# One early sigmoid on ScalarE, into a tile that nothing reads, in a fused linear-attention and gated-MLP kernel

## Chip, cores and metric

The kernel runs on one core of a Trainium2 chip. The time is device microseconds (us) from start to end of one execution; lower is better. Before the change it was 556.48 us, the median of 3 runs (555.26 to 557.22).

## What is computed

```python
# q, k, v, alpha: (4, 8, 768, 48); x below: (3072, 384); w_gate, w_val: (384, 1536); w_out: (1536, 384)
for t in range(S):
    state = alpha[:, :, t, :, None] * state + np.einsum('bhd,bhe->bhde', k[:, :, t], v[:, :, t])
    y[:, :, t] = np.einsum('bhd,bhde->bhe', q[:, :, t], state)
...
gate = 1.0 / (1.0 + np.exp(-(x @ w_gate)))
val = x @ w_val
return (gate * val @ w_out).astype(np.float32)
```

The first loop is a linear attention with decay, by batch and head. Its output, with the heads side by side, is the input x of a gated MLP whose gate is a sigmoid.

## The kernel before, in words

The 3072 tokens are cut into 6 groups of 512 (NG), the 8 heads into 4 pairs (NP): 24 attention units. The MLP's 1536 inner columns are cut into 12 slices of 128 (NF), so there are 6 x 12 = 72 steps. A step of `step(s)` runs 9 gate matmuls, 9 value matmuls (L225: three products of split high and low parts over three tiles of x) and 9 output matmuls into `po` (L643). Between them ScalarE computes `sg`, the sigmoid of the gate sums (L630), VectorE multiplies it into `pv` (L632), ScalarE rounds that to `hh` (L634), and VectorE forms the rest `hl` (L635).

In the first 12 steps the weights come in as well. `weight_piece` loads a piece of raw bits by DMA from the SyncE queue (L345), ScalarE makes two conversions in place (L347, L348), VectorE merges the bits (L351, twice), ScalarE writes the high part of `w` (L353) and VectorE the low part (L355). Raw buffers are used again, so a later L345 waits for an earlier L355. The attention units run in the same stretch: VectorE's scans G and F (L381, L385) and `dec` (L387), GpSimd's products with them (L388, L449), ScalarE's copies `kn` (L404) and sums of |F| (L393), VectorE's states `st` (L489), TensorE's small matmuls (L461, L466, L514, L520).

The order of the work is made ahead of time by the class `Plan`. Every piece of work is added with an engine, an estimated time, a key (a due step, or None) and the names that it reads and writes. `order()` then plays the pieces through and fixes the order in which each engine gets them. Among the pieces that an engine could begin, the one with the smallest rank goes first; the rank comes from the latest time at which a piece may begin:

```python
            by = min((latest[w] - 0.15 - time for w in users[n]), default=float("inf"))
            latest[n] = by if key is None else key * self.STEP if self.parts[n][6] and key > NF + 2 else min(by, key * self.STEP)
        rank = [t - 1000.0 if p[7] else t for t, p in zip(latest, self.parts)]
```

`users[n]` are the pieces that read what piece n writes, `p[7]` is the flag `soon`. On its own engine an instruction never overtakes the one ahead of it.

ScalarE's first piece is `picks` (L321 to L325): a zeroing ACTIVATE (function Copy, L322) and two copies, into `pick`, which TensorE's L508 reads. The functions used on ScalarE are Copy, Abs (L393) and Sigmoid (L630). The program contains two loads of an activation table, put there by the compiler: one ahead of L322, one ahead of the first sigmoid of L630.

The tiles of the pool `sb` are allocated in the order in which the function names them: ... `tiny`, `starts`, four `st`, `sg`, `between`, two `hh`, two `hl`, `every`, `one`.

Of the kernel before, what the change touches and what calls it, by code (L numbers as in the profile page):

```python
# [8 lines left out]
F32 = mybir.dt.float32  # L9
# [5 lines left out]
AF = mybir.ActivationFunctionType  # L15
ALU = mybir.AluOpType

P = 128
# [18 lines left out]
CH, EH = T // C, T // E  # L37
# [162 lines left out]
@with_exitstack  # L200
def gla_then_glu(ctx: ExitStack, tc: tile.TileContext, q, k, v, alpha, rows, vc, vh, weights_in, out):
    nc = tc.nc
    const = ctx.enter_context(tc.tile_pool(name="const", bufs=1))


    ident = const.tile([P, P], F32, name="ident")
    make_identity(nc, ident)
    flags = const.tile([P, NG * NP + 1], F32, name="flags")
    weights = Weights(const)
    within = const.tile([1, 1], I32, name="within")  # L210
    with ExitStack() as fast:
        chunked(fast, tc, rows, vc, vh, weights_in, out, const, ident, flags, weights, within)
        found = nc.values_load(within[0:1, 0:1], min_val=0, max_val=1)
    with tc.If(found < 1):
        general(tc, q, k, v, alpha, out, ident, weights)
# [13 lines left out]
def chunked(ctx, tc, rows, vc, vh, weights_in, out, const, ident, flags, weights, within):  # L229
    nc = tc.nc  # L230
    sb = ctx.enter_context(tc.tile_pool(name="sb", bufs=1))
    ps = ctx.enter_context(tc.tile_pool(name="ps", bufs=1, space=bass.MemoryType.PSUM))
    plan = Plan()
# [56 lines left out]
    d1f = sb.tile([P, T], F32, name="d1f")  # L290
    d1g = {n: sb.tile([P, T], BF16, name=f"d1g{n}") for n in (C, E)}
    mask = {n: sb.tile([P, n], F32, name=f"mask{n}") for n in (C, E)}
    tiny = sb.tile([P, EH], F32, name="tiny")
    starts = sb.tile([P, NG * NP, EH], F32, name="starts")
    sts = [sb.tile([P, EH + 1, D], F32, name=f"st{p}") for p in range(NP)]
    r_x = [const.tile([P, NK, 2, T], F32R, name="x0", tag="x0")]
# [24 lines left out]
    def picks():  # L321
        nc.scalar.activation(out=pick[:, :, 0:D], in_=d1f[:, 0:NK * D].rearrange("p (k m) -> p k m", m=D), func=AF.Copy, scale=0.0)  # L322
        for j in range(2):
            r = slice(R * j, R * j + R)
            nc.scalar.copy(out=pick[r, :, D:R], in_=ident[r, R * j:R * j + D].rearrange("p (k m) -> p k m", m=X16))  # L325

    plan.add("scalar", 0.7, None, picks, writes=[(pickn, "s")])
    plan.add("gpsimd", 1.5, NF - 4.0, later, writes=["later", *(("start", u) for u in range(EARLY))])

# [367 lines left out]
    for s in range(NG * NF):  # L697
        step(s)
        if s in finished:
# [11 lines left out]
                                                               func=AF.Abs, accum_out=flags[:, n_units:n_units + 1]),  # L711
# [6 lines left out]
        out=within, in0=total[1][0:1, 0:1], scalar1=G_BOUND, scalar2=None, op0=ALU.is_le), [total[0]])  # L718
# [150 lines left out]
```

## Time and profile before

| | |
|---|---|
| time, median of 3 runs | 556.48 us |
| range of the 3 runs | 555.26 to 557.22 us |
| time of the profiled execution | 556.98 us |
| its span | 555.3 us |
| instructions in it | 10288 |
| busy: PE / VectorE / ScalarE / GpSimd | 98% / 60% / 33% / 18% |

The profile is one execution taken by the hardware profiler. PE is TensorE's matmuls, PEld its weight loads, DVE VectorE, ACT ScalarE, POOL GpSimd, SP the SyncE queue. A line such as "41.11 0.60 ACT L630 ACTIVATE sg<-pg" gives the start in the span, the duration, the engine, the line of the kernel and the tiles; brackets give the idle time of the engine ahead of it and what ended that.

### The profile page before, as it was taken

To read this page: it belongs to the slowest core of one execution; us is meant where nothing else is said; L and a number is where in the kernel's file an instruction comes from. 1 tells how busy PE (TensorE), PEld (TensorE's weight loads), DVE (VectorE), ACT (ScalarE), POOL (GpSimd) and SP (SyncE) were. 2 spreads that over 40 slices of the span, in tenths; PEclk is the share of its full clock that TensorE was granted. 3 is DMA by queue.
4 is the path that set the end of the run, shared out by engine and by line. 5 is a ranking of instruction groups with operands and counts; after the bars stand their busy time and mean duration, and the time that the engine had idled before them with its cause. 6 is when DMAs were issued, how large, how long until landed. Compare 5 with 4: busy or idle time off the path is not lost.

```text
span 555.3 us, 10288 instructions
## 1 busy us (share of the span) xinstructions
PE 542.1 (98%) x4162; PEld 432.8 (78%) x4162; DVE 335.0 (60%) x648; ACT 183.9 (33%) x334; POOL 100.5 (18%) x133
## 2 busy tenths in 40 slices
PE   8999999999999999999999999999999999999994
PEld 4667776767888888888888888888888888888883
DVE  6889998899858457467467466476475342222221
ACT  2547767652322222322222322222332222221211
POOL 5711222142212112022022022022021010000000
PEclk9999999999999999999999999999999999999998
DMA  8537675644413213324124234024232011100001
GB/s 311 203 102 247 217 228 164 213 132 121 141 31 116 70 45 116 123 48 116 57 59 115 94 79 115 25 92 115 71 102 50 15 28 30 58 0 1 1 1 63
DMA packets 21449, 54.36 MB, mean 98 GB/s; under 512 B 3472, under 2 KB 8592, under 8 KB 21392
## 3 DMA queue, kind: packets, MB, share of 16 engines
q1 hardware_dynamic: 21392, 53.60, 31.6%
q8 instruction: 35, 0.57, 0.4%
q14 instruction: 22, 0.18, 0.1%
HBM read 41.01 MB, written 4.72 MB: 82 GB/s over the span
## 4 chain that ended last, share of the span: by engine, by line
PE 84%; DVE 6%; DMA 4%; ACT 3%; issue 1%; POOL 0%; SPq 0%; DVEq 0%; ACTq 0%; POOLq 0%
PE po L643 24%; PE pv L225 16%; PE pg L225 16%; PE at L225 15%; DMA raw<-in_w_dram 3%; PE pv L614 2%; PE at L560 2%; PE at L400 1%; PE pv L603 1%; PE at L567 1%; DVE w L355 1%; PE pg L603 1%; PE at L603 1%; DVE raw L351 1%; DMA first_w<-in_w_dram 1%
## 5 line engine op out<-in xcount | busy, mean ns | idle before, releaser
L225 PE MATMUL pg<-x,w 128*128 128x512 f32 x477 | 117.4, 390 | 0.0
L643 PE MATMUL po<-hh,w 128*128 128x512 f32 x432 | 115.7, 400 | 1.3 <-ACT hh L634 1.3
L225 PE MATMUL pv<-x,w 128*128 128x512 f32 x459 | 113.4, 391 | 0.7 <-DVE hl L635 0.7
L225 PEld LDWEIGHTS pg<-x,w 128*128 128x128 f32 x477 | 89.1, 188 | 19.1 <-issue 0.4
L225 PEld LDWEIGHTS pv<-x,w 128*128 128x128 f32 x459 | 85.5, 188 | 20.2 <-DVE hl L635 2.0
L643 PEld LDWEIGHTS po<-hh,w 128*128 128x128 f32 x432 | 78.2, 188 | 18.5 <-ACT hh L634 1.9
L225 PE MATMUL at<-x,w 128*128 128x512 f32 x360 | 88.3, 390 | 0.0
L225 PEld LDWEIGHTS at<-x,w 128*128 128x128 f32 x360 | 67.4, 188 | 14.2 <-issue 0.2
L591 POOL TENSOR_TENSOR vs<-st,dec 64x384 f32<-64x384 f32 x32 | 26.4, 827 | 213.0 <-DVE st L586 211.8
L643 PE MATMUL po<-hl,w 128*128 128x512 f32 x216 | 62.0, 392 | 0.0
L632 DVE TENSOR_TENSOR pv<-pv,sg 128x512 f32<-128x512 f32 x32 | 22.3, 697 | 53.9 <-PE pv L225 53.9
L388 POOL TENSOR_TENSOR in<-in,G 128x512 f32<-128x512 f32 x22 | 33.0, 1500 | 90.3 <-DVE G L381 42.1
L632 DVE TENSOR_TENSOR pg<-pg,sg 128x512 f32<-128x512 f32 x21 | 14.7, 699 | 56.2 <-PE pg L225 56.0
L643 PEld LDWEIGHTS po<-hl,w 128*128 128x128 f32 x216 | 40.2, 188 | 9.0 <-issue 0.4
L632 DVE TENSOR_TENSOR at<-at,sg 128x512 f32<-128x512 f32 x19 | 13.3, 699 | 53.0 <-PE at L225 53.0
L586 DVE SCALAR_TENSOR_TENSOR st<-st,dec,at 128x48 f32<-128x48 f32 x128 | 33.9, 265 | 8.4 <-PE at L567 3.0
L630 ACT ACTIVATE sg<-pg 128x512 f32<-128x512 f32 x32 | 19.2, 599 | 57.4 <-PE pg L225 57.4
L634 ACT CAST hh<-pv 128x512 fp32r<-128x512 f32 x32 | 18.9, 589 | 43.1 <-DVE pv L632 43.1
L630 ACT ACTIVATE sg<-at 128x512 f32<-128x512 f32 x21 | 12.6, 600 | 54.8 <-PE at L225 54.8
L630 ACT ACTIVATE sg<-pv 128x512 f32<-128x512 f32 x19 | 11.4, 600 | 52.5 <-PE pv L225 52.5
L381 DVE TENSOR_TENSOR_SCAN G<-in,d1g 128x512 f32<-128x512 f32 x22 | 26.7, 1215 | 2.0 <-DMA in<-in_rows_dram 1.8
L385 DVE TENSOR_TENSOR_SCAN F<-in,d1f 128x512 f32<-128x512 f32 x22 | 27.5, 1251 | 0.5
(158 smaller groups left out, 577.4 us busy)
## 6 DMA issues: line engine op xcount, KB each, us to landing
in<-in_rows_dram SPq DMA_DIRECT2D x16, 516.5 KB, 4.2
raw<-in_w_dram SPq DMA_DIRECT2D x12, 576.0 KB, 5.3
first_w<-in_w_dram SPq DMA_DIRECT2D x10, 576.0 KB, 5.0
x<-yt SPq DMA_DIRECT2D x30, 192.0 KB, 3.4
out_dram<-raw SPq DMA_DIRECT2D x18, 256.0 KB, 2.3
v<-in_vc_dram SPq DMA_DIRECT2D x22, 192.0 KB, 4.6
A<-in_rows_dram SPq DMA_DIRECT2D x32, 128.0 KB, 4.0
in<-in_rows_dram SPq DMA_DIRECT2D x4, 772.5 KB, 5.0
```

Of the source, the lines that this page charges most:

```text
L225: nc.tensor.matmul(out=dst, lhsT=lhs(a, i), rhs=rhs(b, i), start=(n == 0 and i == 0), stop=(n == len(todo) - 1 and i == NK - 1))
L381: plan.add("vector", scan(n), t["G"], lambda: nc.vector.tensor_tensor_scan(out=G[:, ::-1], data0=az[:, n:0:-1], data1=d1g[size], initial=0 ...
L385: plan.add("vector", scan(n), after(t["G"], 0.01), lambda: nc.vector.tensor_tensor_scan(out=F, data0=az[:, 0:n], data1=d1f, initial=0.0, o ...
L388: plan.add("gpsimd", pool_(n), t["kt"], lambda: nc.gpsimd.tensor_tensor(out=kT, in0=kT, in1=G, op=ALU.mult), [gn, (inn, "r")], [(inn, "k")])
L560: nc.tensor.matmul(out=pas[j][1][ro, c // 2 * E:(c // 2 + 1) * E], lhsT=kT[r, cs], rhs=A[r, j, cs], start=True, stop=True)
L586: nc.vector.scalar_tensor_tensor(out=st[:, c + 1, :], in0=st[:, c, :], scalar=dec[:, c:c + 1], in1=pas[c % 2][1][:, T // 2 + c // 2 * D:T ...
L591: plan.add("gpsimd", pool_(EH * D), t["sd"], lambda j=j: nc.gpsimd.tensor_tensor(out=vs[own[j], j], in0=st[own[j], 0:EH], in1=dec[own[j]]. ...
L603: nc.tensor.matmul(out=py[R * j:R * j + D, cs], lhsT=vs[r, j, c, :], rhs=A[r, j, cs], start=True, stop=True)
L630: plan.add("scalar", act(T), None, lambda: nc.scalar.activation(out=sg, in_=got["g"][1][:, 0:T], func=AF.Sigmoid), [got["g"][0]], [sgn], s ...
L632: plan.add("vector", vec(T), None, lambda: nc.vector.tensor_tensor(out=pv, in0=pv, in1=sg, op=ALU.mult), [sgn], [pvn], soon=soon)
L634: plan.add("scalar", act(T), None, lambda: nc.scalar.copy(out=hh, in_=pv), [pvn], [hhn], soon=soon)
L643: nc.tensor.matmul(out=pso_now[m][1][:, 0:T], lhsT=weights.part("o", b, f)[:, m * P:(m + 1) * P], rhs=h[a][:, 0:T], start=(f == 0 and i == ...
```

## The change

A tile `spot` of one column is allocated behind `tiny`, and a piece of work is added to the plan ahead of `picks`: a sigmoid of the first column of the constant tile `tiny` into `spot`, with key None, an estimated time of 0.1, the flag `soon`, and no names read or written. Nothing reads `spot`. All else stays; the lines behind it have numbers that are 1 higher.

```diff
-    tiny = sb.tile([P, EH], F32, name="tiny")
+    tiny, spot = sb.tile([P, EH], F32, name="tiny"), sb.tile([P, 1], F32, name="spot")
...
+    plan.add("scalar", 0.1, None, lambda: nc.scalar.activation(out=spot, in_=tiny[:, 0:1], func=AF.Sigmoid), soon=True)
     plan.add("scalar", 0.7, None, picks, writes=[(pickn, "s")])
```

## Rows read from the trace of the kernel before

**Rows 1.** The profile's page: the chain that ended last, its shares of the span by engine.

```profile
PE 84%; DVE 6%; DMA 4%; ACT 3%; issue 1%; POOL 0%; SPq 0%; DVEq 0%; ACTq 0%; POOLq 0%
```

**Rows 2.** The groups of instructions by line, ScalarE alone: count, busy time and mean ns of one, idle time before them and what ended it.

```profile
L322 ACT ACT_TABLE_LOAD x1 | 1.3, 1283 | 0.8 <-PEq L854 0.8
L630 ACT ACT_TABLE_LOAD x1 | 1.3, 1283 | 0.0
```

**Rows 3.** The chain that ended last, in order of time, around the second table load: start, length, what.

```profile
39.82 1.28 ACT L630
...
41.11 0.60 ACT sg L630
41.71 0.64 ACT raw L347
...
42.35 0.70 DVE pv L632
```

**Rows 4.** The timeline of ScalarE at the start of the span: start, length, instruction, idle time before it.

```profile
0.82 1.28 ACT L322 ACT_TABLE_LOAD   x1 [0.82 <-PEq L854]
2.11 0.32 ACT L322 ACTIVATE first_w<-d1f 128x144 f32<-128x144 f32 x1
2.34 0.45 ACT L325 COPY first_w<-ident 64x48 f32<-64x48 f32 x2
8.63 0.59 ACT L404 COPY kn<-at 128x512 f32<-128x512 f32 x1 [5.83 <-PE at L400]
...
10.31 0.19 ACT L393 ACTIVATION_READ_ACCUMULATOR F<-F 128x1 f32 x1
```

**Rows 5.** The timeline of all engines at the start: the memset of `tiny`, and the first matmuls that read `pick`.

```profile
1.72 0.07 DVE L310 MEMSET tiny<- 128x8 f32 x1
...
16.08 1.08 PE L508 MATMUL pg<-first_w 48*64 48x512 f32 x4
```

**Rows 6.** The timeline of ScalarE around the second table load.

```profile
39.07 0.73 ACT L353 CAST w<-first_w 128x576 fp32r<-128x576 f32 x1
39.82 1.28 ACT L630 ACT_TABLE_LOAD   x1
41.11 0.60 ACT L630 ACTIVATE sg<-pg 128x512 f32<-128x512 f32 x1
41.61 0.74 ACT L347 ACTIVATE raw<-raw 128x576 f32<-128x576 f32 x1
...
42.84 0.54 ACT L353 CAST w<-first_w 128x384 fp32r<-128x384 f32 x1
43.27 0.60 ACT L634 CAST hh<-pv 128x512 fp32r<-128x512 f32 x1
44.38 0.60 ACT L630 ACTIVATE sg<-pg 128x512 f32<-128x512 f32 x1 [0.51 <-PE pg L225]
```

**Rows 7.** The timeline of all engines in the same stretch: TensorE's, VectorE's and GpSimd's instructions, and the next load that SyncE issues.

```profile
37.19 2.30 PE L225 MATMUL pg<-x,w 128*128 128x512 f32 x9
...
39.91 2.34 PE L225 MATMUL pv<-x,w 128*128 128x512 f32 x9
...
40.87 3.55 SPq L345 DMA_DIRECT2D first_w<-in_w_dram  x2
...
41.89 0.53 DVE L351 SCALAR_TENSOR_TENSOR first_w<-first_w 128x384 uint32<-128x384 uint32 x1
42.05 1.52 POOL L449 TENSOR_TENSOR in<-in,F 128x512 f32<-128x512 f32 x1 [7.08 <-DVE F L385]
42.08 2.20 PE L225 MATMUL pg<-x,w 128*128 128x512 f32 x9
42.35 0.70 DVE L632 TENSOR_TENSOR pv<-pv,sg 128x512 f32<-128x512 f32 x1
42.96 0.64 DVE L387 TENSOR_TENSOR dec<-in,G 128x4 f32<-128x4 f32 x1
43.52 0.55 DVE L355 TENSOR_TENSOR w<-first_w,w 128x384 fp32r<-128x384 f32 x1
...
45.31 1.66 PE L643 MATMUL po<-hh,w 128*128 128x512 f32 x6
```

**Rows 8.** The timeline of VectorE: the same `dec` instruction with no GpSimd product beside it.

```profile
89.43 0.13 DVE L387 TENSOR_TENSOR dec<-in,G 128x4 f32<-128x4 f32 x1
```

**Rows 9.** The timeline of TensorE behind that stretch: the first instruction up to 135 us that has idle time ahead of it, and the four with the most.

```profile
54.24 1.66 PE L643 MATMUL po<-hh,w 128*128 128x512 f32 x6 [0.17 <-ACT hh L634]
56.20 2.33 PE L225 MATMUL pv<-x,w 128*128 128x512 f32 x9 [0.31 <-DVE hl L635]
...
88.05 0.56 PE L466 MATMUL at<-v,kn 128*48 128x48 f32 x16 [1.39 <-ACT kn L404]
...
108.94 0.73 PE L643 MATMUL po<-hh,w 128*128 128x512 f32 x2 [1.12 <-ACT hh L634]
...
119.98 0.66 PE L400 MATMUL at<-ident,in 128*128 128x128 f32 x4 [0.78 <-DVE st L489]
```

**Rows 10.** The page's costliest groups: the matmuls that read `hh`, `hl` and x, with count, busy time and mean ns of one.

```profile
L225 PE MATMUL pg<-x,w 128*128 128x512 f32 x477 | 117.4, 390 | 0.0
L643 PE MATMUL po<-hh,w 128*128 128x512 f32 x432 | 115.7, 400 | 1.3 <-ACT hh L634 1.3
...
L643 PE MATMUL po<-hl,w 128*128 128x512 f32 x216 | 62.0, 392 | 0.0
```

## The prediction

> **What bounds the kernel now.** I read the chain that ended last first, by engine and then in order of time around the second table load; then the table loads among ScalarE's groups; then the timelines of ScalarE, and of all engines in the same microseconds; last TensorE's idle times behind them. TensorE makes up 84% of the chain [rows 1], and it is in effect the bound: behind about 55 us it has few gaps and those are short [rows 9]. So whatever ScalarE saves counts only if it makes one of those gaps shorter, or if it starts a transfer or another engine earlier that does.
>
> ScalarE loads an activation table twice, at 0.82 us ahead of the zeroing of `pick`, and at 39.82 us ahead of the first sigmoid of the MLP, 1.28 us each [rows 2, 4, 6]. There is no third: the Copy and Abs work behind 39.82 runs on the table that the sigmoid asked for. The chain in order of time runs straight through the second load: load, sigmoid, L347, then VectorE's product L632 [rows 3]. Taken by itself that view says that 1.28 us of the span hang on the load. A chain names one releaser for each step, though, and not how far ahead the next-latest one was; that has to be read from the timelines of the neighbours [rows 7].
>
> **The change, part by part.**
>
> *Where the new sigmoid goes.* The rank of a piece is its latest start, less 1000 with `soon`. The new piece has key None and nobody uses what it writes, so its latest start is infinite, and infinite less 1000 is infinite. `picks` has users (L508 reads `pick`, and the chain of users ends in step 0 with key 0), so its rank is finite. Both can begin at once, so `picks` goes first. By this reading the sigmoid is not ScalarE's first instruction but the first one behind `picks`. The first load stays at 0.82 us, for Copy; the second moves from 39.82 us to the end of `picks`, 2.34 + 0.45 = 2.79 us [rows 4]. The number of loads is then two, as before. The rest of the plan stays as it is: the new piece takes 0.1 us of the plan's time on an engine that has nothing else ready there, reads and writes no name, and so displaces nothing.
>
> *What it adds at the start.* A load, 1.28 us, and a sigmoid of 128x1. No such sigmoid is in the trace; the nearest rows are a 128x1 instruction on ScalarE, 0.19 us, and an ACTIVATE of 128x144, 0.32 us [rows 4]. I take 0.2, the one-column row being nearest. The end is 2.79 + 1.28 + 0.2 = 4.3 us, 4.4 with the larger price. The next thing ScalarE does begins at 8.63 us, after 5.83 us of idling for TensorE [rows 4], so 4.2 us of cover are left. `tiny` is filled at 1.79 us, before the sigmoid can start, and `pick` is not read before 16.08 us [rows 5]. If the sigmoid did come first, the load would be the one at 0.82 us and `picks` would end 0.2 to 0.3 us later, still 13 us ahead of its reader. Cost on the path: 0 either way. A gain here is excluded too, as ScalarE is idle there already.
>
> *What it takes away at 39.82 us.* The load, 1.28 us. The cast ahead of it ends at 39.80 and the sigmoid starts at 41.11 [rows 6]; neighbours without a load overlap by 0.10 (the sigmoid runs 41.11 to 41.71, the next starts at 41.61), so ScalarE gets back 1.31 + 0.10 = 1.41 us. The sigmoid's input is there: the gate matmuls end at 37.19 + 2.30 = 39.49 [rows 7]. So it would start near 39.7. Now each thing that follows:
> - L632 waits for the value matmuls, whose end is 39.91 + 2.34 = 42.25, and stands on VectorE behind L351, which ends at 42.42 (instructions there overlap by some 0.07). It starts at 42.35 now [rows 7] and will then: gain 0.
> - L353 of `first_w` (42.84 now) needs that L351, so it starts at 42.45 at the earliest: up to 0.4 us gained on ScalarE. Its reader on VectorE, L355 at 43.52, stands behind `dec` L387, which takes 0.64 there against 0.13 alone [rows 7, 8] and ends at 43.60 as GpSimd's L449 ends at 43.57. That product was released by scan F, not by ScalarE. Gain for L355: 0. The load that SyncE issues behind it, whose issue ends at 40.87 + 3.55 = 44.42 [rows 7], does not move either.
> - `hh` L634 (43.27 now) needs L632, 42.35 + 0.70 = 43.05: 0.2 us gained. Its reader L643 starts at 45.31 because TensorE works through from 42.08 to there, 1.4 us after `hh` is done at 43.87 [rows 6, 7]. Gain: 0.
> - The second sigmoid waits for the gate matmuls, 42.08 + 2.20 = 44.28, after 0.51 us of idling [rows 6, 7]. It starts at 44.38 before and after. From there ScalarE is where it was.
>
> So the 1.41 us go into ScalarE's own waits between 39.8 and 44.4 us; at 44.38 the idle time is that much more and nothing has moved. TensorE's first gap behind this, 0.17 us at 54.24 [rows 9], is ten microseconds later.
>
> The rows show 1283 ns for a load and 1.31 us between the neighbours, with nothing else in it [rows 2, 6]. The Trainium skill, page "ScalarE: Activation LUTs", section "What ACT_TABLE_LOAD costs", counts a drain of 1380 ns on top and 2.66 us in all for a switch of sets. This trace does not show that drain. By the page ScalarE would get back 2.66 us instead of 1.41, and if all of that reached the end the time would be about 553.8 us. That lies with rival 2, whose chance holds it.
>
> *Sum.* Profiled execution: span 555.3, of which 0 goes and 0 comes; with the 1.7 us around the span that is 556.98 again. The median of the runs shown is 0.5 us below the profiled one, so 556.5 us. The bounds of the unknown part are 0 and 1.41 us gained.
>
> **Rivals.**
> 1. *The chain is right.* The load is on the path and all of the 1.41 us reach the end: 556.48 - 1.41 = 555.1 us, 0.25% less. For it: the chain view [rows 3]. Against it: four followers that are held by something else [rows 7], and a step of ScalarE that TensorE resets at 44.38 [rows 6].
> 2. *More than the load's row.* A slightly different timing in the first 12 steps lets TensorE's later gaps close. The five gaps listed sum to 0.17 + 0.31 + 1.39 + 1.12 + 0.78 = 3.8 us [rows 9]; half of that gives 554.6 us. For it: two of the largest wait for ScalarE. Against it: nothing of this change is left at 44.38 us that could reach them.
> 3. *Slower by placement.* `spot` is allocated between `tiny` and `starts`, so `sg`, `hh` and `hl` lie elsewhere. TensorE reads `hh` and `hl` in 432 + 216 = 648 matmuls all through the kernel. If the new place cost each of them the 10 ns by which the mean of those with `hh` (400) now exceeds those with x (390) [rows 10], that would be 6.5 us: 563.0. It decides the sign from 1.67 / 648 = 2.6 ns upwards. Against it: `hl` lies directly behind `hh` and reads at 392, so no place in this pool is seen to be dear, and a longer mean need not be a longer pace.
> 4. *The change doesn't do what it says.* Either the sigmoid stands behind `picks` (which I expect, and which is in the forecast), or a load is still made at L630: then 556.5 us, with 1.3 to 1.6 us more of ScalarE's idle start in use. Against the latter: only one load was made for 72 sigmoids with Copy and Abs between them [rows 2].
>
> **How the numbers follow.** About 0.3%, 1.67 us, is what a measurement of this kernel can tell from no change. Forecast (nothing reaches the end): 0.79. Rival 1: 0.08. Rival 2: 0.05. Rival 3: 0.06. Rival 4 with a load left at L630: 0.02. The forecast, rival 1 and rival 4 are all within 0.3%: 0.79 + 0.08 + 0.02 = 0.89. Faster is rival 2, 0.05; slower is rival 3, 0.06. The range takes in the full 1.41 us at its lower end, 555.0, and at the upper end as much as the runs shown differ among themselves above their median, some 1 us: 557.5. The cases outside it hold 0.11, and the spread of medians some more.
>
> **What would show it.** In the profile after: a table load at about 2.8 us behind `picks`, one at 0.82, none at L630; the first sigmoid of the MLP near 39.7 us; L632 still at 42.35, L355 still at 43.5, the second sigmoid still at 44.38 with TensorE's matmuls named as the releaser; TensorE's gaps at 54, 56, 88, 109 and 120 us as before; the matmuls that read `hh` and `hl` with means of 400 and 392. If the sigmoid stands first, there is one load in all and my reading of the rank is wrong, at no cost in time. If L632 or L355 moves ahead by a microsecond, the sum is wrong and rival 1 takes over; if the mean of L643 grows, rival 3.

## The result and the profile after

The changed kernel takes 561.0 us (median of 10 runs, 560.65 to 562.4) against 556.98 us for the kernel before (10 runs, 555.26 to 560.36): a ratio of 1.0078, 95% interval 1.0062 to 1.0095. It is slower, by some 4 us, and outside the forecast range. The profiled execution's span is 559.7 us, 4.4 more than before. TensorE's granted clock is 0.997 of full speed (the 2.4 GHz level) in both profiled executions, so the clock isn't the reason.

Everything that was forecast for ScalarE happened. The groups of ScalarE by line, then its timeline at the start (answers to [rows 2, 4]):

```profile
L322 ACT ACT_TABLE_LOAD x1 | 1.3, 1283 | 0.8 <-PEq L855 0.8
L327 ACT ACT_TABLE_LOAD x1 | 1.3, 1283 | 0.0
```

```profile
2.34 0.46 ACT L325 COPY first_w<-ident 64x48 f32<-64x48 f32 x2
2.81 1.28 ACT L327 ACT_TABLE_LOAD   x1
4.11 0.20 ACT L327 ACTIVATE spot<-tiny 128x1 f32<-128x1 f32 x1
9.28 0.58 ACT L405 COPY kn<-at 128x512 f32<-128x512 f32 x1 [4.97 <-PE at L401]
```

The sigmoid stands behind `picks`, not ahead of it; the load at L630 is gone, one at 2.81 us has come. Now the place where the load was, from the timeline of all engines (answers to [rows 6, 7]). This execution runs 0.65 us late from the first microseconds on, because 13 warm-up matmuls took 4.25 us (second fence) instead of 3.60, so 0.65 is to be taken off. It isn't the loss: the kernel e2 below, with the time of before, starts about as late (`kn` at 9.14 us; 8.63 before, 9.28 here).

```profile
40.35 0.61 ACT L631 ACTIVATE sg<-pg 128x512 f32<-128x512 f32 x1
...
42.37 0.75 ACT L348 ACTIVATE raw<-raw 128x576 f32<-128x576 f32 x1 [1.41 <-DMA raw<-in_w_dram]
...
43.00 0.70 DVE L633 TENSOR_TENSOR pv<-pv,sg 128x512 f32<-128x512 f32 x1
...
44.20 0.56 DVE L356 TENSOR_TENSOR w<-first_w,w 128x384 fp32r<-128x384 f32 x1
...
45.03 0.60 ACT L631 ACTIVATE sg<-pg 128x512 f32<-128x512 f32 x1 [0.38 <-PE pg L225]
```

```profile
4.55 4.25 PE L615 MATMUL pv<-ident 128*128 128x512 bf16 x13
```

The first sigmoid starts at 39.70 on the old scale instead of 41.11, VectorE's product at 42.35 as before, L356 at 43.55 (43.52), the second sigmoid at 44.38 as before, released by TensorE. The 1.41 us went into a wait of 1.41 us for a raw piece: the conversion behind the sigmoid (L347, now L348), which the prediction's list of followers left out, starts at 41.72 on the old scale against 41.61.

The loss is elsewhere. The page's costliest groups (answers to [rows 10]):

```profile
L225 PE MATMUL pg<-x,w 128*128 128x512 f32 x477 | 118.0, 392 | 0.0
L644 PE MATMUL po<-hh,w 128*128 128x512 f32 x432 | 117.5, 404 | 0.4 <-ACT hh L635 0.4
...
L644 PE MATMUL po<-hl,w 128*128 128x512 f32 x216 | 63.4, 397 | 0.0
```

The output matmuls take 4 and 5 ns more, those with x 1 to 2. By the pages the busy time grew by 1.8 us (hh), 1.4 us (hl) and 2.0 us (x: pg, pv, at), 5.2 us in all. TensorE's timeline of one step in the last group, first before, then after:

```profile
488.46 1.52 PE L643 MATMUL po<-hh,w 128*128 128x512 f32 x6
489.82 0.84 PE L643 MATMUL po<-hl,w 128*128 128x512 f32 x3
490.50 2.20 PE L225 MATMUL pv<-x,w 128*128 128x512 f32 x9
492.54 2.20 PE L225 MATMUL at<-x,w 128*128 128x512 f32 x9
494.58 1.52 PE L643 MATMUL po<-hh,w 128*128 128x512 f32 x6
```

```profile
486.43 1.56 PE L644 MATMUL po<-hh,w 128*128 128x512 f32 x6
487.83 0.86 PE L644 MATMUL po<-hl,w 128*128 128x512 f32 x3
488.53 2.24 PE L225 MATMUL at<-x,w 128*128 128x512 f32 x9
490.61 2.20 PE L225 MATMUL pg<-x,w 128*128 128x512 f32 x9
492.65 1.56 PE L644 MATMUL po<-hh,w 128*128 128x512 f32 x6
```

From start to start a step takes 6.12 us before and 6.22 after. The differences of the starts give its blocks: six matmuls with `hh` 1.36 and 1.40, three with `hl` 0.68 and 0.70, the next nine with x 2.04 and 2.08, the last nine 2.04 and 2.04. No gap and no wait is in it: the matmuls themselves follow each other more slowly. TensorE's gaps behind 50 us are in sum no larger than before (answers to [rows 9]; the one of 0.17 at 54.24 is gone, one of 0.34 at 63.93 is new):

```profile
56.65 2.35 PE L225 MATMUL pv<-x,w 128*128 128x512 f32 x9 [0.30 <-DVE hl L636]
63.93 0.56 PE L467 MATMUL at<-v,kn 128*48 128x48 f32 x16 [0.34 <-ACT kn L405]
88.68 0.56 PE L467 MATMUL at<-v,kn 128*48 128x48 f32 x16 [1.14 <-ACT kn L405]
109.00 0.73 PE L644 MATMUL po<-hh,w 128*128 128x512 f32 x2 [0.43 <-ACT hh L635]
120.40 0.65 PE L401 MATMUL at<-ident,in 128*128 128x128 f32 x4 [1.09 <-DVE st L490]
```

At 120.40 the changed kernel is 0.4 us behind (119.98 before). From there the lag grows step by step. The first output matmuls of the 13th and of the last step, first before, then after:

```profile
149.00 1.52 PE L643 MATMUL po<-hh,w 128*128 128x512 f32 x6
...
545.94 0.62 PE L643 MATMUL po<-hh,w 128*128 128x512 f32 x2
```

```profile
149.44 1.56 PE L644 MATMUL po<-hh,w 128*128 128x512 f32 x6
...
551.04 0.63 PE L644 MATMUL po<-hh,w 128*128 128x512 f32 x2
```

The lag is 0.44 us at the 13th step and 5.10 us at the last, 0.08 us a step. What stands behind the last matmul takes some 0.6 us less than before, which leaves the 4.4 us of the span.

### The profile page after: what moved, and what is told of

The parts are those of the page before. It is cut to its first block, busy times and chain, and to the rows that moved or that the text cites. A ratio compares the mean times of both kernels' runs of the same rounds, so it can differ in the third digit from the quotient of the medians.

```text
span 559.7 us, 10289 instructions
## 1 busy us (share of the span) xinstructions
PE 547.8 (98%) x4162; PEld 433.3 (77%) x4162; DVE 335.3 (60%) x648; ACT 183.7 (33%) x335; POOL 102.1 (18%) x133
## 4 chain that ended last, share of the span: by engine, by line
PE 89%; DVE 4%; ACT 3%; DMA 2%; issue 1%; POOL 0%; DVEq 0%; ACTq 0%; POOLq 0%
PE po L644 25%; PE pg L225 17%; PE pv L225 17%; PE at L225 15%; PE pv L615 2%; PE at L561 2%; PE at L401 1%; DMA raw<-in_w_dram 1%; PE pv L604 1%; DMA first_w<-in_w_dram 1%; PE at L568 1%; PE at L604 1%; PE pg L604 1%; DVE w L356 1%; PE pg L521 1%
## 5 line engine op out<-in xcount | busy, mean ns | idle before, releaser
L644 PE MATMUL po<-hh,w 128*128 128x512 f32 x432 | 117.5, 404 | 0.4 <-ACT hh L635 0.4
L644 PE MATMUL po<-hl,w 128*128 128x512 f32 x216 | 63.4, 397 | 0.0
```

The costliest lines, as they stand in the source:

```text
L644: nc.tensor.matmul(out=pso_now[m][1][:, 0:T], lhsT=weights.part("o", b, f)[:, m * P:(m + 1) * P], rhs=h[a][:, 0:T], start=(f == 0 and i == ...
```

## The experiments

Theory: `spot`, which takes 32 bytes of the pool in each partition (one column holds 4; the kernel e3 bears the 32 out), moves `hh` and `hl` 32 bytes further on, and that alone slows TensorE. Rival: the early sigmoid, its table load or the added instructions do it. All edits below are to the kernel before, unless the changed kernel is named. "Step" is the start to start of a step in the last group, read as above.

**The tile without the sigmoid (e1).**

```diff
-    tiny = sb.tile([P, EH], F32, name="tiny")
+    tiny, spot = sb.tile([P, EH], F32, name="tiny"), sb.tile([P, 1], F32, name="spot")
```

> The kernel before with the one-column tile allocated between tiny and starts, and no sigmoid into it: starts, st, sg, hh and hl lie 32 bytes further on, the program's instructions are those of before. Placement theory: the whole loss is here, about 561 us (ratio 1.007 to 1.009), the output matmuls that read hh with a mean of 404 ns and those that read hl with 397 ns, and the step's first nine matmuls behind them slow as well. Rival (the moved table load or the added instructions slow TensorE): the time of before, about 557 us, means of 400 and 392 ns.

561.67 us, ratio 1.0083 (1.0059 to 1.0106), step 6.22. The whole loss is here, with the instructions of before.

**The sigmoid without the shift (e2).** In the changed kernel `spot` is allocated behind `hl`.

```diff
+    spot = sb.tile([P, 1], F32, name="spot")   # behind r_hh, r_hl; no longer beside tiny
```

> The changed kernel with the one-column tile allocated behind hh and hl: the early sigmoid and the moved table load are there, and starts, st, sg, hh and hl lie where they lay before. Placement theory: the time of before, about 557 us (ratio 0.997 to 1.001), means of 400 and 392 ns, second table load at 2.8 us. Rival (the sigmoid or its load): about 561 us and means of 404 and 397 ns.

556.78 us, ratio 1.0002 (0.9986 to 1.0018), step 6.12, loads at 0.82 and 2.81 us. The rival falls, and the change as forecast, without its side effect, is worth nothing that can be measured.

**hh and hl back, sg and st still moved (e3)**, in the changed kernel; **hh and hl alone moved (e4)**, in the kernel before.

```diff
-    sb.tile([P, 40], F32, name="between")
+    sb.tile([P, 32], F32, name="between")   # changed kernel
...
+    sb.tile([P, 48], F32, name="between")   # kernel before
```

> The changed kernel with the spacer tile ahead of hh cut from 40 to 32 columns: hh and hl are back where they lay before, while starts, st and sg stay 32 bytes further on. Placement theory in the form that hh and hl alone matter: about 557 us, means of 400 and 392 ns. In the form that sg, starts or st matter: about 561 us. Rival (the sigmoid or its load): 561 us.

> The kernel before with the spacer tile ahead of hh grown from 40 to 48 columns: hh and hl lie 32 bytes further on as in the changed kernel, all else is that of before. Placement theory in the form that hh and hl alone matter: about 561 us, means of 404 and 397 ns. In the form that sg, starts or st matter, and by the rival: about 557 us.

557.24 us, ratio 0.9999 (0.9983 to 1.0016), step 6.12; and 561.39 us, 1.0087 (1.0064 to 1.011), step 6.22. The place of `hh` and `hl` is necessary and enough. In e3 eight columns, 32 bytes, undo what the one-column tile did.

**Everything moved by 32 bytes (e5); hh and hl moved by 64 (e6).**

```diff
+    const.tile([P, 8], F32, name="ahead")   # ahead of ident: all tiles move
     ident = const.tile([P, P], F32, name="ident")
...
-    sb.tile([P, 40], F32, name="between")
+    sb.tile([P, 56], F32, name="between")   # the other kernel
```

> The kernel before with an unused 32-byte tile allocated ahead of everything: x, the weights, sg, hh and hl all lie 32 bytes further on and keep their distances. Theory A (the absolute place of a moving operand decides, at a multiple of 64 bytes it is dear): hh, hl and x are all at such places, so at least 561 us, and all matmuls of a step with a longer pace than 227 ns. Theory B (the distance of hh and hl to x or to the weights decides): about 557 us, pace 227 ns.

> The kernel before with the spacer grown from 40 to 56 columns: hh and hl lie 64 bytes further on, all else as before. Theories A and B with a period of 64 bytes: about 557 us, means of 400 and 392 ns. If any new place is dear, or only the distance that before has is cheap: about 561 us or more.

557.38 us, 1.0007 (0.999 to 1.0023), step 6.12; and 561.27 us, 1.0079 (1.0061 to 1.0098), step 6.21. The absolute place doesn't count (theory A falls), the distance to something that moved along does; and it doesn't repeat after 64 bytes.

**hl alone by 32 (e7); hh by 32 with hl by 64 (e8).**

```diff
-    r_hh, r_hl = ring("hh", 2, T, dtype=F32R), ring("hl", 2, T, dtype=F32R)
+    r_hh = ring("hh", 2, T, dtype=F32R)
+    sb.tile([P, 8], F32, name="apart")   # the second kernel has "between" at 48, too
+    r_hl = ring("hl", 2, T, dtype=F32R)
```

> The kernel before with 8 unused columns between hh and hl: hl alone lies 32 bytes further on. If each matmul pays by the place of its own moving operand: the three matmuls of a step with hl take some 20 ns more in all, and what follows them some part of the 38 ns that the nine behind them lost, so 558 to 560 us, with the mean of those with hh at 400 ns and with hl near 397. If the nine x matmuls are slowed by the hl ahead of them, all of their loss is here too.

> The kernel before with the spacer grown from 40 to 48 columns and 8 unused columns between hh and hl: hh lies 32 bytes further on, hl 64. With a period of 64 bytes hh alone is at a dear place: the six matmuls of a step with hh take some 25 to 45 ns more, 558 to 560 us, mean 404 for hh and 392 for hl. If the place of hh matters not at all and the loss comes from hl: about 557 us.

559.13 us, 1.0039 (1.0019 to 1.006), step 6.17: blocks of 1.36, 0.71, 2.06 and 2.04. And 560.64 us, 1.0066 (1.0046 to 1.0086), step 6.20: 1.41, 0.68, 2.07, 2.04. TensorE's timeline with `hl` alone moved:

```profile
489.72 1.52 PE L645 MATMUL po<-hh,w 128*128 128x512 f32 x6
491.08 0.86 PE L645 MATMUL po<-hl,w 128*128 128x512 f32 x3
491.79 2.23 PE L225 MATMUL pv<-x,w 128*128 128x512 f32 x9
493.85 2.20 PE L225 MATMUL at<-x,w 128*128 128x512 f32 x9
495.89 1.52 PE L645 MATMUL po<-hh,w 128*128 128x512 f32 x6
```

Each block pays by the place of its own operand, and three slow matmuls with `hl` are enough to slow some of the nine behind them. The second of the two kernels doesn't isolate `hh`, as I had meant, and came out above the 558 to 560 us expected: 64 bytes are no cheap distance either.

**The distance to what? Half of the weights moved (e9).** x, `hh`, `hl` and the weights of slices 6 to 11 stay, those of slices 0 to 5 lie 32 bytes further on. All tiles of the pool `sb` that are allocated ahead of `between`, `sg` and `st` among them, move along; steps of both halves use them alike.

```diff
     r_x = [const.tile([P, NK, 2, T], F32R, name="x0", tag="x0")]
+    const.tile([P, 8], F32, name="ahead")
...
-    sb.tile([P, 40], F32, name="between")
+    sb.tile([P, 32], F32, name="between")
```

> The kernel before with an unused 32-byte tile behind x0 and the spacer cut to 32 columns: the weights of slices 0 to 5 lie 32 bytes further on; x, hh, hl and the weights of slices 6 to 11 lie where they lay. Theory W (the distance of a moving operand to the weights that are loaded beside it decides): the steps of slices 0 to 5 are slow in all 27 matmuls, those of slices 6 to 11 at 227 ns, so the time lies near 560 us and half the steps take at least 6.2 us against 6.12. Theory X (the distance of hh and hl to x decides): all steps as before, about 557 us.

562.03 us, 1.0095 (1.0069 to 1.0121), 2 us more than expected. TensorE's timeline, a step of the first half of the slices and one of the second half:

```profile
498.28 1.56 PE L644 MATMUL po<-hh,w 128*128 128x512 f32 x6
499.68 0.86 PE L644 MATMUL po<-hl,w 128*128 128x512 f32 x3
500.38 2.26 PE L225 MATMUL pg<-x,w 128*128 128x512 f32 x9
502.48 2.26 PE L225 MATMUL pv<-x,w 128*128 128x512 f32 x9
504.58 1.56 PE L644 MATMUL po<-hh,w 128*128 128x512 f32 x6
...
529.77 1.52 PE L644 MATMUL po<-hh,w 128*128 128x512 f32 x6
531.13 0.84 PE L644 MATMUL po<-hl,w 128*128 128x512 f32 x3
531.81 2.20 PE L225 MATMUL pv<-x,w 128*128 128x512 f32 x9
533.85 2.20 PE L225 MATMUL at<-x,w 128*128 128x512 f32 x9
535.89 1.52 PE L644 MATMUL po<-hh,w 128*128 128x512 f32 x6
```

6.30 us against 6.12 in one execution, all four blocks longer (1.40, 0.70, 2.10, 2.10). Between the two halves only the place of the weights differs. So what counts is the distance between the operand that streams through a matmul and the weights (theory W); theory X falls.

While a matmul runs, TensorE loads the weights of the next (below, the load for the first x matmul starts at 475.01, beside the last matmul with `hl`, which starts at 475.00). Those in use and those being loaded lie at the same place within 256 bytes almost everywhere, so the times hardly tell which of the two count. A border between the halves does, a little:

```profile
474.55 0.85 PE L644 MATMUL po<-hl,w 128*128 128x512 f32 x3
475.24 2.26 PE L225 MATMUL pv<-x,w 128*128 128x512 f32 x9
```

These three matmuls with `hl` use weights that stayed (slice 10), and the next nine use weights that moved (slice 0). The three take 0.69 us and not 0.68, and 0.69 again at the next such border, at 480.80. That speaks for the weights being loaded; it is 0.01 us, and no version was made to test it.

**The period: 256 bytes further on (e10), 128 further on (e11), 128 back (e12).**

```diff
-    sb.tile([P, 40], F32, name="between")
+    sb.tile([P, 104], F32, name="between")   # 72 and 8 in the other two
```

> The kernel before with the spacer grown to 104 columns: hh and hl lie 256 bytes further on, which puts them at the same place as x and the weights within 512 bytes (before: 256 apart). If the distance counts within 256 bytes: about 557 us and a step of 6.12 us. If only the old place is cheap: about 561 us.

> The kernel before with the spacer grown to 72 columns: hh and hl lie 128 bytes further on. If the distance counts within 128 bytes: about 557 us. If it counts within 256 or more: 560 to 562 us, with a step of 6.2 us.

> The kernel before with the spacer cut to 8 columns: hh and hl lie 128 bytes further to the front. With a distance that counts within 256 bytes: the same pace of each of the 27 matmuls as with 128 bytes further on. With a longer period: another pattern.

556.86 us, 0.9999 (0.9982 to 1.0015), step 6.12; 559.51 us, 1.0042 (1.0024 to 1.0059), step 6.20; 560.59 us, 1.0059 (1.0034 to 1.0085), step 6.20. The steps with 128 either way agree to 0.01 us in each block, and 256 costs nothing: the distance counts within 256 bytes. The first of the two 128s came out half a microsecond below what was expected. That the distance is 0 in the kernel before is worked out from the kernel's tiles, in the order of their allocation, each rounded up to 32 bytes and the pool `sb` behind the one of x and the weights; no trace shows addresses. The first weights lie 12288 bytes behind `x0` and `hh` 123648 bytes behind those, which is 48 and 483 times 256; the tiles of x, of the weights, of `hh` and of `hl`, and the parts of them that a matmul reads, are multiples of 256 bytes long.

The steps by distance (in bytes; blocks and step in us), each from the timeline of TensorE as above:

```
distance of hh, hl to the weights     hh x6   hl x3   next x9  last x9  step
0 (before, e2, e3, e5) and 256 (e10)  1.36    0.68    2.04     2.04     6.12
32 (after, e1, e4)                    1.40    0.70    2.08     2.04     6.22
64 (e6)                               1.39    0.69    2.09     2.04     6.21
128 (e11)                             1.39    0.71    2.06     2.04     6.20
-128 (e12)                            1.39    0.70    2.07     2.04     6.20
```

## Why the prediction was wrong

- *What bounds the kernel*: right. TensorE's pace sets the end, and with a longer step (6.12 to 6.22) and gaps that are in sum no larger the span grew.
- *Where the sigmoid goes*: right, behind `picks`, two loads. The chain view named 1.28 us that were not to be had; the neighbours' timelines said so, and the kernel with the sigmoid and no shift shows it (1.0002, and at the least 0.9986, while a gain of 1.28 us would be 0.9977).
- *What it adds at the start*: right; 0.20 us for the sigmoid, and 4.97 us of idling were still left for cover.
- *Sum*: 0 for these terms, right. It left out the allocation: I listed it as rival 3, with a chance of 0.06, and not as a part of the change with bounds of its own. The range therefore ended at 557.5, though the rival's own price reached to 563.0.
- *The step that failed* is the evidence against rival 3: "`hl` lies directly behind `hh` and reads at 392, so no place in this pool is seen to be dear". `hh` and `hl` lie multiples of 2048 bytes apart, so they have the same place within 256 bytes, as x has. At other places they were dear: moved by 32 bytes they take 404 and 397 ns, and the step 0.10 us more. Those rows were three measurements of one and the same distance, and no evidence on any other. That the mean of 400 need not be a longer pace was right: in the last group of the kernel before six of them take 1.36 us, 227 ns each, like those with x.
- *Rival 3's price* was 10 ns for each of 648 matmuls, 6.5 us. It was 0.06 us a step on those nine (6.7 ns each) and 0.04 us on the nine x matmuls behind them, which I had not thought of. 0.10 us in 72 steps would be 7.2 us; the span shows 4.4. In the first 12 steps, where TensorE still waits for others, no lag builds up (it goes from 0.65 to 0.44 us). In a step right behind the attention's small matmuls the six with `hh` take 1.49 us before already (463.85 to 465.34) and 1.50 after (467.67 to 469.17), and the step loses 0.07 (6.25 and 6.32). That the price had the right order is in part luck: it had too many ns for each matmul, too few matmuls and too many steps.
- *What would show it* did its work: "if the mean of L643 grows, rival 3". Of its other signs, those of ScalarE and VectorE came; TensorE's gaps did not stay "as before".

Why the nine x matmuls behind a slow block are slow too, though their own operands lie as before, stays open. In the kernel before, at distance 0, the six with `hh` behind the attention's matmuls are longer too (1.49 us against 1.36); whether that is the same thing isn't shown. Why the distance counts at all stays open too; that the two reads contend for something in the memory or the engine is a conjecture. No version here beats the kernel before: 6.12 us a step is the least that any of them shows.

## What to carry to other kernels

A new tile is part of a change even if nothing reads it: list which tiles it moves, and who streams them. Where TensorE is the bound, compare the places of the streamed operands and of the weights within 256 bytes (in this kernel, the same place was the fastest of those tried), and test an edit with its tile allocated last, so that its own worth is seen. And rows in which the suspected quantity never varied are no evidence against it.

## What was not expected of the hardware

A matmul of 128x512 f32 follows the one before after 227 ns (2.04 us for nine) when its streamed operand and the weights have a distance of 0 within 256 bytes, and after 230 to 237 ns at the other distances tried (0.69 us to 0.71 for three); the weight loads keep their 188 ns in the page's rows of both kernels. With the weights themselves moved, all 27 matmuls of a step are slow, 6.30 us. The Trainium skill, page "TensorE: Matmul & The Clock Gate", section "Step-by-step: what each phase is for", says that loading the next weights doesn't steal read bandwidth from the running matmul, each having a read port of its own. Here the running matmuls are up to 4% slower (0.71 us against 0.68) by where the weights lie relative to their operand, with the weights' own loads no longer. That is hard to square with the sentence, though no run shows what they contend for; the measurement decides.
